# Sliding-window attention, channel mix and gated conv in one launch: seven quarter products for `val`, and the conv's fifth tap by an accumulating DMA

## The chip, the cores and the metric

One core of one Trainium2 chip runs the whole program in one launch. The metric is the device time of the launch in microseconds, the median over several executions. Before the change it is 450.53 us (three executions, 449.9 to 452.18).

## What is computed

Batch 4, 576 tokens a sequence, 8 heads of 64, so rows of 512 numbers. All inputs and outputs are fp32.

```
attn = softmax(q k^T / 8, only the last 64 positions) v          # 4 x 8 x 576 x 64
x    = attn with its heads side by side                          # 4 x 576 x 512
xk   = mu_k * x + (1 - mu_k) * x_prev;  xr likewise with mu_r
h    = relu(xk @ w_k) ** 2                                       # 512 -> 1024
x2   = sigmoid(xr @ w_r) * (h @ w_v)                             # 1024 -> 512
gate = sigmoid(sum over k = 0..4 of conv_w[k] * x2 shifted by 4 - k tokens)
out  = (gate * (x2 @ w_val)) @ w_out                             # both 512 x 512
```

## The kernel before, in words

**Products.** A product of fp32 data is made of three matmuls of fp32r: every operand is split into a high part (a copy in fp32r) and a low part (the operand less its high part), and high x high, low x high and high x low are added up in PSUM. The splits are `split` (high part on ScalarE, L410, or as a cast on VectorE, L411; low part on VectorE, L413) and, for weights, `weight` (L224, L225, L227); a weight comes as 64-bit words that `words` (L198 to L203) turns into fp32 first. All products of 128x512 weights and activations go through `gemm` (L426).

**Stages.** The 2304 tokens of the four sequences stand one behind another and are cut in five blocks (256, then four of 512). Attention works on 20 units (a block and a pair of heads); block by block follow the mix `xm` (L380 to L396), `r_tile` (r, then the sigmoid, L513), `h_pair` (h, relu L472, square L496 and L501, low part L503) and `v_tile`, whose result is multiplied by r (L526) and stored to `x2d` in DRAM (L527). Attention of the next block runs between the products of this one. The last part, called the tail here, takes the sequences one by one: `load` brings x2 of a sequence back as `xb` (L537, issued by SyncE), `prep` splits its two halves of 288 tokens, `gate` makes the conv and its sigmoid, `val_pair` the product with w_val (two banks of 128x288 in a call) and its product with the gate (`gv`, L595), which is split again, `out_pair` the product with w_out, the copy to SBUF (L612) and the store (L613). The four taps k = 1 to 4 are VectorE's (L565), tap 0 is ScalarE's (L563). `xb` and `gate` are double buffered: xb2 takes xb0's place, xb3 that of xb1.

**Order.** Nothing runs in the order in which the code names it. Every step is an entry of `Plan` (L50) with a key, an engine, a cost in ns, a rank and the keys it waits for; `Plan.run` sorts them by rank (the tables RANK and ADJ), picks step after step for the engine that could start first, and so writes one fixed instruction queue for each engine. `any` (L68) lets the planner choose between ScalarE and VectorE. On the chip each queue runs strictly in order. So a change of one cost or one table entry can move instructions anywhere in the program.

Of the kernel before, what the change touches and what calls it, by code (L numbers as in the profile page):

```python
# [19 lines left out]
P = 128  # L20
# [21 lines left out]
ADJ = {('exp', 7): 265, ('mask', 15): -40, ('r', 0, 3): -195, (('w_v', 3), 't'): -390, ('h', 2, 1): 40,  # L42
# [4 lines left out]
       ('eps', 5): 250, ('tp', 4): 100, ('rec', 1): 540, ('mask', 10): -250}  # L47


class Plan:  # L50
# [21 lines left out]
    def run(self):  # L72
# [49 lines left out]
def tile_kernel(ctx, tc, qkh, vh, mu, conv, w_k, w_v, w_r, w_val, w_out, out):  # L122
# [17 lines left out]
    sb = ctx.enter_context(tc.tile_pool(name="sb", bufs=2))  # L140
    sb4 = ctx.enter_context(tc.tile_pool(name="sb4", bufs=4))
# [3 lines left out]
    wr = [w1.tile([P, NF, DM], F32R, name=f"wr{i}") for i in range(2)]  # L145
# [18 lines left out]
    plan = Plan(pg=4, pq=1, pa=2, pb=2, pc=2)  # L164
# [41 lines left out]
    def weight(key, rank, w_dram, dst, nm, bufs, prev=None, sprev=None, after=(), free=(), later=None, used=(), queue="dma"):  # L206
# [11 lines left out]
        else:  # L218
# [7 lines left out]
        op((key, "lo"), "dve", v_ns(n), later, [(key, "hi")],  # L226
           lambda: V.tensor_tensor(out=dst[1], in0=s(), in1=f32(dst[0]), op=ALU.subtract))  # L227
# [9 lines left out]
    def unit(u, r):  # L237
# [14 lines left out]
        def half(tag, shape):  # L252

            if t:
                return tile_(at2, tag, shape)
            if hp % 2 == 0:
                Q["half", tag] = tile_(at2, tag, shape)
            return Q["half", tag][:, hp % 2 * shape[1] // 2:]
# [102 lines left out]
    def wide_x():  # L361
        x = [sbx.tile([P, NF, TB], F32R, tag="x", name=f"x{i}") for i in range(4)]
        for t in range(1, NB):
            X[t] = dict(k=x[:2], r=x[2:])

    def mix(t, g, w, r):
# [8 lines left out]
        def scaled():  # L375

            m = M[k] = sb.tile([P, 2, TB], F32, tag="xm", name=f"xm{t}_{g}{w}") if t else X[0][w][:, 2 * g:2 * g + 2]
# [3 lines left out]
        def scaled_v():  # L381
            m = M[k] = sb.tile([P, 2, TB], F32, tag="xm", name=f"xm{t}_{g}{w}") if t else X[0][w][:, 2 * g:2 * g + 2]
# [23 lines left out]
    def split(key, r, deps, n, src, dst):  # L406
# [5 lines left out]
        op((lo, *key[1:]), "dve", v_ns(n), r + 1, [(hi, *key[1:])],  # L412
           lambda: V.tensor_tensor(out=dst(1), in0=src(), in1=f32(dst(0)), op=ALU.subtract))  # L413
# [44 lines left out]
    def h_pair(t, p, r):  # L458
# [4 lines left out]
        for i in range(2):  # L463
# [3 lines left out]
            def relu(e, i=i):  # L467
                if i == 0:
                    Rk[t, p] = sb.tile([P, 2, TB], F32, tag="rk", name=f"rk{t}_{p}")
# [24 lines left out]
        def hi():  # L494
# [7 lines left out]
        op(("slo", t, p), "dve", v_ns(2 * n), r + 2 * d + 4, [("sq", t, p)],  # L502
           lambda: V.tensor_tensor(out=Ss[t][1][:, f, :n], in0=rk(), in1=f32(Ss[t][0][:, f, :n]), op=ALU.subtract))  # L503

    def r_tile(t, m, r):
# [5 lines left out]
        def sig():  # L511
            Sg[t, m] = sb4.tile([P, TB], F32, tag="sg", name=f"sg{t}_{m}")
# [18 lines left out]
    Xb, Gt, Gv, Vg = {}, {}, {}, {}  # L531

    def load(b, r):
# [5 lines left out]
        last = [("x2lo", b - 2, h) for h in range(2)] + [("tap", b - 2, f, TAPS - 1) for f in range(NF)] if b >= 2 else []  # L539
# [3 lines left out]
    def prep(b, h, r):  # L543

        x = lambda i: X[NB - 1]["kr"[h]][i][:, :, :HS]
        src = lambda: Xb[b][:, :, GAP + h * HS:GAP + (h + 1) * HS]
        last = [("val", b - 1, h, p) for p in range(2)] if b else [("h", NB - 1, m) for m in range(NFF)] if h == 0 \
            else [("r", NB - 1, m) for m in range(NF)]
        split(("x2", b, h), r, [("ldx", b), *last], NF * HS, src, x)

    def gate(b, r):
# [3 lines left out]
        last = [("gv", b - 2, h, p) for h in range(2) for p in range(2)] if b >= 2 else []  # L555
        op(("gbuf", b), "none", 0, r, [("ldx", b), *last], buffer)

        def tap(f, k):
# [5 lines left out]
            else:  # L564
                V.scalar_tensor_tensor(out=g, in0=src, scalar=c, in1=g, op0=ALU.mult, op1=ALU.add)  # L565
        for p in range(2):
            for k in range(TAPS):
                for f in range(2 * p, 2 * p + 2):
                    op(("tap", b, f, k), *(("dve", v_ns(S) + 70) if k else ("act", a_ns(S) + 90)), r + 10 * p,
                       [("gbuf", b), "wc"] + ([("tap", b, f, k - 1)] if k else []), lambda f=f, k=k: tap(f, k))  # L570
            op(("gate", b, p), "act", a_ns(2 * S), r + 10 * p + 5, [("tap", b, f, TAPS - 1) for f in (2 * p, 2 * p + 1)],
               lambda p=p: ACT.activation(out=Gt[b][:, 2 * p:2 * p + 2, :], in_=Gt[b][:, 2 * p:2 * p + 2, :],
                                          func=AF.Sigmoid), table="sig")

    def pair2(key, r, p, m0, x, deps, freed, pool, ring):
# [8 lines left out]
    def val_pair(b, h, p, r):  # L584
        f = slice(2 * p, 2 * p + 2)
        q = 4 * b + 2 * h + p
        name = lambda k, q: (k, q // 4, q // 2 % 2, q % 2)
        pair2(("val", b, h, p), r, p, 0, lambda: [X[NB - 1]["kr"[h]][i][:, :, :HS] for i in range(2)],
              lambda i: [("x2lo", b, h), (("w_val", 2 * p + i), "lo")], ("gv", b, h, p), "pb", "pb")

        def gv():
            if p == 0:
                Gv[b, h] = Q["g", h]
            Vg[b, h, p] = sb.tile([P, 2, HS], F32, tag="xm", name=f"gv{b}_{h}{p}")
            V.tensor_tensor(out=Vg[b, h, p], in0=Ps["val", b, h, p][:, :, :HS],  # L595
                            in1=Gt[b][:, f, h * HS:(h + 1) * HS], op=ALU.mult)
        op(("gv", b, h, p), "dve", v_ns(2 * HS), r + 12,
           [("val", b, h, p), ("gate", b, p), "turn_s", *([name("gv", q - 1)] if q else []),
            *([name("glo", q - 2)] if q >= 2 else [])], gv)
        last = [("out", b - 1, h, q) for q in range(2)] if b else []  # L600
        split(("g", b, h, p), r + 13, [("gv", b, h, p), *last], 2 * HS, lambda: Vg[b, h, p],
              lambda i: Gv[b, h][i][:, f, :])

    def out_pair(b, h, p, r):
        pair2(("out", b, h, p), r, p, NF, lambda: Gv[b, h],
              lambda i: [("glo", b, h, 0), ("glo", b, h, 1), (("w_out", 2 * p + i), "lo")], ("o", b, h, p), "pc", "pc")
        q = 4 * b + 2 * h + p

        def store():
            o = sb.tile([P, 2, HS], F32, tag="rk", name=f"o{b}_{h}{p}")  # L610
# [39 lines left out]
    def staging():  # L650
# [3 lines left out]
        Q["raw"] = [sbx.tile([P, 2048], I32, tag="x", name=f"raw{i}") for i in range(2)] \  # L654
            + [a[:, 1].bitcast(I32) for a in (xr, sr)]
        two = [sbx.tile([P, 2, 1024], F32, tag="x", name=f"s_{i}") for i in range(2)]
        Q["sw"] = [two[i][:, j] for i in range(2) for j in range(2)]
# [17 lines left out]
    def turn():  # L675
# [3 lines left out]
        Q["raw2"] = [own.tile([P, 1024], I32, name=f"rawb{i}") for i in range(2)]  # L679
        Q["s2"] = [own.tile([P, 512], F32, name=f"sb_{i}") for i in range(2)]  # L680
        Q["pb"] = ctx.enter_context(tc.tile_pool(name="pb", bufs=2, space=PSUM, side="right"))

    def turn_s():
# [3 lines left out]
        for i in range(2):  # L687
            Q["g", i] = [own.tile([P, NF, HS], F32R, name=f"g{i}{c}") for c in "hl"]
        Q["pc"] = ctx.enter_context(tc.tile_pool(name="pc", bufs=2, space=PSUM))
# [5 lines left out]
    pieces2 = [(n, p) for n in ("w_val", "w_out") for p in range(4)]  # L695
    for i, (name, p) in enumerate(pieces2):
        w, m = {"w_val": (w_val, 0), "w_out": (w_out, DM)}[name]
        c = P * p
# [74 lines left out]
```

## Time and profile before

| | |
|---|---|
| median of three executions | 450.53 us |
| the profiled execution's own time | 449.83 us |
| its span, first to last instruction | 448.0 us |
| busy: TensorE / VectorE / ScalarE / GpSimd | 430.7 / 304.5 / 241.5 / 17.0 us |
| matmuls of the tail (val, out) | 384 + 384, of 128x288 |
| tail, from the first val matmul to the end | 341.63 to 448.0 us |

The profile is of one execution, which lasted 449.83 us, of which 448.0 us lie between its first and its last instruction. "PE" is TensorE, "DVE" VectorE, "ACT" ScalarE, "POOL" GpSimd, "SP" SyncE. Busy time is a sum over the span; what ends an engine's idle time is named behind an arrow. A row of a timeline merges neighbours of one kind (x84: 84 instructions), and its duration then runs from the first start to the last end. Instructions overlap at their ends, so the step from one start to the next is shorter than the duration of one.

### The profile page before, as it was taken

The page shows a single profiled execution, that of the slowest core. Times are in us where ns is not written, and L with a number is a line of the kernel's source. Part 1 is how long each engine was busy: PE and PEld are TensorE (multiplying, and loading weights), DVE is VectorE, ACT ScalarE, POOL GpSimd, SP SyncE. Part 2 cuts the span into 40 slices and gives each one's busy share as a digit, 9 for nine tenths or more (in the row PEclk, how much of TensorE's full clock was granted, in tenths as well). Part 3 has the DMA queues.
Part 4 walks back from the last instruction along what each step waited for, and adds up shares of the span by engine and source line. Part 5 has one row for each costly group of instructions (what it writes and reads, how often), then busy time and mean ns, then how long its engine had stood idle before and what let it go on. Part 6 is the DMA issues. An engine that isn't in the chain of part 4 may idle for free.

```text
span 448.0 us, 7939 instructions
## 1 busy us (share of the span) xinstructions
PE 430.7 (96%) x3220; PEld 369.5 (82%) x3220; DVE 304.5 (68%) x438; ACT 241.5 (54%) x546; POOL 17.0 (4%) x67
## 2 busy tenths in 40 slices
PE   6889899889999999999999989999999999999996
PEld 4668788668878888888888878888889999999996
DVE  3999899978497149597254266999111999998130
ACT  4799898768555358697239553297100353413121
POOL 2011000001000001001000000000000000000000
PEclk9989999999999999999999999999999999999999
DMA  8996733601131152221120008241133004010122
GB/s 311 407 341 236 283 102 122 214 6 47 48 105 44 72 171 65 89 90 49 47 95 1 0 1 292 96 128 60 22 132 126 28 29 159 26 54 26 48 87 105
DMA packets 16116, 48.90 MB, mean 109 GB/s; under 512 B 1872, under 2 KB 2640, under 8 KB 14800
## 3 DMA queue, kind: packets, MB, share of 16 engines
q1 hardware_dynamic: 15216, 42.10, 27.3%
q10 hardware_dynamic: 864, 6.29, 3.7%
q8 instruction: 25, 0.41, 0.4%
q14 instruction: 11, 0.09, 0.1%
HBM read 38.95 MB, written 9.44 MB: 108 GB/s over the span
## 4 chain that ended last, share of the span: by engine, by line
PE 80%; DVE 12%; DMA 4%; ACT 1%; issue 1%; POOL 0%; ACTq 0%; SPq 0%; POOLq 0%; DVEq 0%
PE h L426 20%; PE v L426 19%; PE out L426 11%; PE val L426 9%; PE r L426 9%; PE qk L277 4%; PE at L343 3%; PE at L330 3%; DMA raw<-w_v 2%; PE r L444 2%; DMA xb<-x2d 1%; DVE s L322 1%; DVE x L413 1%; DVE s L289 1%; DVE s L203 1%
## 5 line engine op out<-in xcount | busy, mean ns | idle before, releaser
L426 PE MATMUL h<-x,wk 128*128 128x512 f32 x384 | 91.0, 393 | 0.0
L426 PEld LDWEIGHTS h<-x,wk 128*128 128x128 f32 x384 | 71.1, 188 | 14.7
L426 PE MATMUL v<-sh,wv 128*128 128x512 f32 x256 | 80.7, 391 | 0.0
L313 ACT ACTIVATE s<-s,m 128x128 f32<-128x128 f32 x144 | 55.7, 388 | 14.6 <-DVE m L307 14.6
L426 PEld LDWEIGHTS v<-sh,wv 128*128 128x128 f32 x256 | 48.1, 188 | 10.2 <-issue 0.2
L426 PE MATMUL val<-x,wk 128*128 128x288 f32 x384 | 53.0, 294 | 0.3 <-DVE gv L595 0.3
L426 PEld LDWEIGHTS val<-x,wk 128*128 128x128 f32 x384 | 51.4, 188 | 0.8 <-DVE gv L595 0.6
L426 PE MATMUL v<-sl,wv 128*128 128x512 f32 x128 | 49.9, 389 | 0.0
L565 DVE SCALAR_TENSOR_TENSOR gate<-xb,wc,gate 128x576 f32<-128x576 f32 x64 | 48.6, 812 | 1.6 <-ACT gate L563 1.6
L426 PE MATMUL r<-x,wr 128*128 128x512 f32 x192 | 47.0, 397 | 0.0
L426 PEld LDWEIGHTS r<-x,wr 128*128 128x128 f32 x192 | 35.2, 188 | 8.1 <-DVE x L413 0.4
L526 DVE TENSOR_TENSOR sg<-v,sg 128x512 f32<-128x512 f32 (+1 forms) x20 | 12.7, 635 | 38.9 <-PE v L426 36.7
L289 DVE SCALAR_TENSOR_TENSOR s<-qk,cap 128x1024 f32<-128x1024 f32 (+1 forms) x24 | 22.5, 952 | 14.7 <-PE qk L277 9.5
L472 ACT ACTIVATE rk<-h 128x512 f32<-128x512 f32 (+1 forms) x36 | 19.9, 556 | 22.4 <-PE h L426 21.9
L503 DVE TENSOR_TENSOR sl<-rk,sh 128x1024 fp32r<-128x1024 f32 x16 | 19.6, 1222 | 15.4 <-ACT rk L501 15.2
L612 ACT ACTIVATE o<-out 128x576 f32<-128x576 f32 (+1 forms) x17 | 10.4, 618 | 36.0 <-PE out L426 26.0
L563 ACT ACTIVATE gate<-xb,wc 128x576 f32<-128x576 f32 x16 | 11.3, 766 | 31.8 <-DMA xb<-x2d 30.7
L426 PEld LDWEIGHTS v<-sl,wv 128*128 128x128 f32 x128 | 24.0, 188 | 4.8
L426 PE MATMUL out<-g0h,wk 128*128 128x288 f32 x128 | 27.4, 295 | 0.0
L330 PE MATMUL at<-ident,s 128*128 128x128 f32 x144 | 22.8, 282 | 4.3 <-DVE s L322 3.2
L313 ACT ACTIVATION_READ_ACCUMULATOR s<-s,m 128x1 f32 x144 | 26.9, 187 | 0.0
L426 PE MATMUL out<-g1h,wk 128*128 128x288 f32 x128 | 26.6, 295 | 0.0
(112 smaller groups left out, 675.2 us busy)
## 6 DMA issues: line engine op xcount, KB each, us to landing
qk<-qk SPq DMA_DIRECT2D x16, 544.0 KB, 4.9
vt<-vh SPq DMA_DIRECT2D x16, 512.0 KB, 4.3
xb<-x2d SPq DMA_DIRECT2D x4, 1152.0 KB, 5.8
out_t<-o SPq DMA_DIRECT2D x15, 288.0 KB, 2.1
x2d<-sg SPq DMA_DIRECT2D x16, 256.0 KB, 2.0
raw<-w_r SPq DMA_DIRECT2D x2, 1024.0 KB, 8.4
raw<-w_k ACTq DMA_DIRECT2D x2, 1024.0 KB, 7.9
raw<-w_v ACTq DMA_DIRECT2D x2, 1024.0 KB, 8.2
```

The lines of the kernel that those rows point to most:

```text
L277: PE.matmul(a["ps"][heads[c % 2], h, c // 2 * P:c // 2 * P + P], lhsT=a["q"][heads[h], c * W:(c + 1) * W], rhs=a["k"][heads[h], c * W:c * ...
L289: V.scalar_tensor_tensor(out=o, in0=ps[:, i:i + j], scalar=D ** -0.5, in1=cap[:, None, :].to_broadcast([P, j, P]), op0=ALU.mult, op1=ALU.min)
L313: ACT.activation(out=s, in_=s, func=AF.Exp, bias=l(0)[:, c:c + 1], accum_out=l(1)[:, c:c + 1])
L330: PE.transpose(a["tp", h][:, c * P:(c + 1) * P], a["s"][:, h * n2 + c, :], ident)
L343: PE.matmul(a["o"][heads[h], c * W:(c + 1) * W], lhsT=a["v"][:, c, heads[h]], rhs=a["pt"][:, h, c * W:(c + 1) * W], start=True, stop=True)
L426: PE.matmul(ps, lhsT=a, rhs=b[:, kt, :], start=(kt == 0 and i == 0), stop=(kt == nk - 1 and i == 2))
L472: ACT.activation(out=o, in_=ps, func=AF.Relu)
L503: lambda: V.tensor_tensor(out=Ss[t][1][:, f, :n], in0=rk(), in1=f32(Ss[t][0][:, f, :n]), op=ALU.subtract))
L526: V.tensor_tensor(out=s, in0=Ps["v", t, m][:, :n], in1=s, op=ALU.mult)
L563: ACT.activation(out=g, in_=src, func=AF.Copy, scale=c)
L565: V.scalar_tensor_tensor(out=g, in0=src, scalar=c, in1=g, op0=ALU.mult, op1=ALU.add)
L612: ACT.activation(out=o[:, i], in_=Ps["out", b, h, p][:, i, :HS], func=AF.Copy)
```

## The change

(a) **val by seven products of quarters.** Per sequence, x2 (its halves of 288 tokens by its two 256-wide halves of features) and w_val are cut in quarters; four sums of x quarters and four differences of weight quarters are formed, and seven quarter products (12 matmuls of 128x288 each) replace the eight of before: 84 matmuls a sequence in place of 96. Two PSUM banks collect them: `u` takes m1, m6, m7 and m4 one on top of the other, `v` takes m2, then m5, then m3. After m1, m6 and m7 the running sum in `u` is copied to SBUF by ScalarE (L684), and VectorE adds it to what `v` holds (`valc`, L713) before the product with the gate (`gv`, L715); the quarter that needs no copy is multiplied straight from PSUM (L718). The splits of a sequence are five in place of two: one 1152 wide, four 576 wide, behind the four sums (L594, high parts L601 on ScalarE or L602 on VectorE, low parts L604). w_val comes in two pieces with four differences of 256 each.

(b) **The fifth tap of sequences 1 to 3** (k = 4): ScalarE scales it into `tt` (L632, two instructions of 576 for each half of the features), and a DMA issued by GpSimd adds the 128x1152 of `tt` (576 KB) to `gate` (L643), six in all. It waits for tap 0 of both features. The taps of VectorE (L626) that follow wait for the DMA. They go from 64 to 52.

(c) w_out goes to the place of w_r instead of beside w_val; the staging tiles are merged. The helper `vg` puts the low parts and sums on VectorE (no step of before's splits changes its engine by it). RANK and ADJ have new numbers, and the planner adds a small bias against VectorE, so the whole order is made anew.

TensorE has 2498 matmuls in place of 2546. The core of the diff (constants, storage and the weight pieces cut):

```diff
+        for p in range(2):
+            fs = (2 * p, 2 * p + 1)
+            for f in fs:
+                op(("tap", b, f, 0), "act", a_ns(S) + 90, r + 10 * p, [("gbuf", b), "wc"], lambda f=f: tap(f, 0))
+            d = [("tap", b, f, 0) for f in fs]
+            for k in by:
+                op(("part", b, p, k), "act", 2 * a_ns(S) + 180, r + 10 * p + 1,
+                   ["turn_s", ("gbuf", b), "wc", *([parts[-2]] if len(parts) > 1 else [])], lambda p=p, k=k: part(p, k))
+                parts.append(("acc", b, p, k))
+                op(parts[-1], "pool", 1000, r + 10 * p + 1, [("part", b, p, k), *d], lambda p=p, k=k: G.dma_start(
+                    out=Gt[b][:, 2 * p:2 * p + 2, :], in_=Z[b, p, k], accum_op=ALU.add), moves=3500)
+                d = [parts[-1]]
...
+        product(0, "m1", A11, B11, "u", True, [], fin(1, 0))
+        copy(0, "m1", 0)
+        product(1, "m2", A12, B21, "v", True, [], fin(0, 0))
+        use(0, 0, r + 7, lambda: Zv("v"), lambda: U[mul, b, 0], [key("m2"), (mul + "u", b, 0)])
+        product(2, "m6", S2, T2, "u", False, [(mul + "u", b, 0), key("m1")])
+        copy(1, "m6", 2)
+        product(3, "m5", S1, T1, "v", True, [], fin(0, 1))
+        product(4, "m7", S3, T3, "u", False, [(mul + "u", b, 1), key("m6")])
+        copy(2, "m7", 4)
+        use(1, 1, r + 25, lambda: Zv("v"), lambda: U[mul, b, 2], [key("m5"), (mul + "u", b, 2)])
+        product(5, "m4", A22, T4, "u", False, [(mul + "u", b, 2)])
+        use(1, 0, r + 31, lambda: Zv("u"), None, [key("m4")])
+        product(6, "m3", S4, B22, "v", False, [fin(1, 1)])
+        use(0, 1, r + 37, lambda: Zv("v"), lambda: U[mul, b, 1], [key("m3"), (mul + "u", b, 1)])
...
+            if u:
+                op(("valc", b, h, p), "dve", v_ns(QN), r, deps,
+                   lambda: V.tensor_tensor(out=u(), in0=ps(), in1=u(), op=ALU.add))
+                vg(("gv", b, h, p), QN, r + 1, [("valc", b, h, p), ("gate", b, p)],
+                   lambda E: E.tensor_tensor(out=g(), in0=u(), in1=g(), op=ALU.mult))
...
-                gemm(Ps[key][:, i, :HS], wk, x(), m0 + 2 * p + i, range(NF), NF)
+                gemm(Ps[key][:, i, :HS], wr, x(), m0 + 2 * p + i, range(NF), NF)
```

Three places of the new order matter for what follows.

ScalarE, where val of the first sequence runs and the second sequence's xb arrives. Before (`gate_3147` is gate1, `xb_3090` xb1):

```order
L513 ACTIVATE sg_3_2963<-r_3_2934 128x512
L563 ACTIVATE gate_3147<-xb_3090,wc 128x576 x3
L410 ACTIVATE g0h<-gv_01_3151 128x576
L563 ACTIVATE gate_3147<-xb_3090,wc 128x576
L410 ACTIVATE g1h<-gv_10_3183 128x576
```

After (`val0m_3006` is bank u of the first sequence, `gate_3097` gate1, `xb_3037` xb1, `xt` the sums):

```order
L601 ACTIVATE x<-xt 128x576 x2
L684 ACTIVATE sgs<-val0m_3006 128x576 x2
L624 ACTIVATE gate_3097<-xb_3037,wc 128x576 x2
L601 ACTIVATE x<-xt 128x576
L684 ACTIVATE sgs<-val0m_3006 128x576
L632 ACTIVATE tt_04_3105<-xb_3037,wc 128x576 x2
L624 ACTIVATE gate_3097<-xb_3037,wc 128x576
```

The copies after m1 and m6 stand ahead of two scalings of xb1 and of a split of a sum of xb1; the copy after m7 stands behind them.

SyncE, at the end of the channel mix. Before, the load of the third sequence (`xb_2966`) stands ahead of the last four stores of x2:

```order
L537 DMA xb_2966<-x2d 128x4x576
L527 DMA x2d<-sg_0_2916 128x512
L527 DMA x2d<-sg_1_2932 128x512
L527 DMA x2d<-sg_2_2947 128x512
L527 DMA x2d<-sg_3_2963 128x512
L537 DMA xb_3090<-x2d 128x4x576
```

After, the same load (`xb_2977`) stands between them, two stores ahead of xb1's (`xb_3037`):

```order
L232 DMA st<-w_out 128x1024 x4
L540 DMA x2d<-sgs 128x512 x2
L569 DMA xb_2977<-x2d 128x4x576
L540 DMA x2d<-sgs 128x512 x2
L569 DMA xb_3037<-x2d 128x4x576
```

It has moved behind two stores, and on VectorE behind the sums of xb0 that it overwrites.

VectorE, where val of the second sequence has begun (after; `gate_2615` is gate0, `val1m` belongs to the second sequence, `xb_2977` is xb2; x2: two of a kind):

```order
L715 TENSOR_TENSOR gate_2615<-sgs,gate_2615 128x2x288
L713 TENSOR_TENSOR sgs<-val1m_3162,sgs 128x576
L604 TENSOR_TENSOR x<-xt,x 128x576
L604 TENSOR_TENSOR x<-xb_2977,x 128x1152
L594 TENSOR_TENSOR xt<-xb_2977 128x576
L426 TENSOR_TENSOR g0l<-gate_2615,g0h 128x576
L594 TENSOR_TENSOR xt<-xt,xb_2977 128x576
L604 TENSOR_TENSOR x<-xt,x 128x576
L713 TENSOR_TENSOR sgs<-val1m_3198,sgs 128x576
L604 TENSOR_TENSOR x<-xt,x 128x576
L426 TENSOR_TENSOR g1l<-gate_2615,g1h 128x576 x2
L626 SCALAR_TENSOR_TENSOR gate_3097<-xb_3037,wc,gate_3097 128x576
```

The last row is the first tap of gate1, of feature block 2, and the first instruction that waits for an accumulating DMA. It stands 26 instructions behind xb1's cast; before, the first two taps of gate1 stood five behind it. The two scalings (L632) that its half of gate1 waits for are ScalarE's eleventh and twelfth instruction behind the copy after m7.

## Rows read from the trace of the kernel before

**Rows 1.** The page, parts 1 and 2: busy times, and TensorE's granted clock by slices.

```profile
PE 430.7 (96%) x3220; PEld 369.5 (82%) x3220; DVE 304.5 (68%) x438; ACT 241.5 (54%) x546; POOL 17.0 (4%) x67
...
PEclk9989999999999999999999999999999999999999
```

**Rows 2.** Stretches: span, busy us (count) of PE, PEld, DVE, ACT, POOL; clock, DMA.

```profile
80.00:100.00 20.00, 16.73 (x170) 13.27 (x164) 17.41 (x25) 15.49 (x45) 1.05 (x7) 1.00 0.38 123
100.00:260.00 160.00, 160.00 (x1194) 130.63 (x1192) 94.77 (x133) 97.34 (x235) 6.27 (x16) 1.00 0.21 65
...
309.00:341.70 32.70, 32.70 (x146) 27.09 (x145) 8.24 (x10) 5.49 (x8) 0.12 (x1) 1.00 0.17 61
341.70:353.20 11.50, 11.16 (x86) 10.93 (x84) 6.85 (x10) 3.39 (x6) 0.11 (x1) 1.00 0.38 127
353.20:444.30 91.10, 91.07 (x684) 90.72 (x684) 65.45 (x91) 27.89 (x37) 0.11 (x1) 1.00 0.16 60
```

**Rows 3.** The chain of work that ended last: start, us, engine and work.

```profile
339.88 1.99 DMA x2d<-sg
342.96 5.93 DMA xb<-x2d
...
421.87 22.41 PE out L426 x168
```

**Rows 4.** TensorE's timeline where the tail begins: start, us, work, idle before.

```profile
341.63 11.22 PE L426 MATMUL val<-x,wk 128*128 128x288 f32 x84
353.19 5.00 PE L426 MATMUL val<-x,wk 128*128 128x288 f32 x36 [0.34 <-DVE gv L595]
```

**Rows 5.** VectorE's timeline, 348.99 to 352.38 and 404.34 us.

```profile
348.99 0.76 DVE L411 CAST x<-xb 128x1152 fp32r<-128x1152 f32 x1 [0.38 <-DMA xb<-x2d]
349.67 0.75 DVE L595 TENSOR_TENSOR gv<-val,gate 128x576 f32<-128x576 f32 x1
350.33 1.35 DVE L413 TENSOR_TENSOR x<-xb,x 128x1152 fp32r<-128x1152 f32 x1
...
404.34 5.91 DVE L565 SCALAR_TENSOR_TENSOR gate<-xb,wc,gate 128x576 f32<-128x576 f32 x8
```

**Rows 6.** ScalarE's timeline, 348.98 to 351.58 us.

```profile
348.98 2.11 ACT L563 ACTIVATE gate<-xb,wc 128x576 f32<-128x576 f32 x3 [28.31 <-DMA xb<-x2d]
351.00 0.67 ACT L410 ACTIVATE g0h<-gv 128x576 fp32r<-128x576 f32 x1
351.58 0.76 ACT L563 ACTIVATE gate<-xb,wc 128x576 f32<-128x576 f32 x1
```

**Rows 7.** SyncE's timeline: issue of loads and stores.

```profile
322.30 0.53 SPq L537 DMA_DIRECT2D xb<-x2d  x1
329.01 13.90 SPq L527 DMA_DIRECT2D x2d<-sg  x4
```

**Rows 8.** VectorE's groups by shape: count, then busy us and mean ns of one.

```profile
L565 DVE SCALAR_TENSOR_TENSOR gate<-xb,wc,gate 128x576 f32<-128x576 f32 x64 | 48.6, 812 | 1.6 <-ACT gate L563 1.6
L413 DVE TENSOR_TENSOR g1l<-gv,g1h 128x576 fp32r<-128x576 f32 x8 | 6.0, 755 | 0.6 <-ACT g1h L410 0.5
L411 DVE CAST g0h<-gv 128x576 fp32r<-128x576 f32 x5 | 2.2, 455 | 9.1 <-PE out L426 9.1
```

**Rows 9.** DMA issues: KB each, median us from issue to landing.

```profile
xb<-x2d SPq DMA_DIRECT2D x4, 1152.0 KB, 5.8
...
raw<-w_r SPq DMA_DIRECT2D x2, 1024.0 KB, 8.4
...
rawb<-w_out SPq DMA_DIRECT2D x4, 512.0 KB, 3.4
```

**Rows 10.** GpSimd's timeline: the same copy of two numbers a partition, twice.

```profile
65.25 0.24 POOL L419 COPY xT<-xT 128x2 f32<-128x2 f32 x1 [6.63 <-DVE xm_0k L396]
...
106.38 1.38 POOL L419 COPY xT<-xT 128x2 f32<-128x2 f32 x1 [6.27 <-DVE xm_0k L396]
```

**Rows 11.** VectorE's timeline at the second of these.

```profile
106.50 1.22 DVE L413 TENSOR_TENSOR x<-xm_0r,x 128x1024 fp32r<-128x1024 f32 x1
```

More of the change, by code (lines that the diff above doesn't have):

```diff
@@ L554, in buffer @@
             Gt[b] = Q["own", b % 2].tile([P, NF, S], F32, tag="gate", name=f"gate{b}")
-        last = [("gv", b - 2, h, p) for h in range(2) for p in range(2)] if b >= 2 else []
+        last = [("glo", b - 2, h, p) for h in range(2) for p in range(2)] if b >= 2 else []
         op(("gbuf", b), "none", 0, r, [("ldx", b), *last], buffer)
@@ L565, in tap, with part @@
                 V.scalar_tensor_tensor(out=g, in0=src, scalar=c, in1=g, op0=ALU.mult, op1=ALU.add)
-        for p in range(2):
[L567 to L571, printed above, removed]
+        def part(p, k):
+            t = Z[b, p, k] = Q["tt"].tile([P, 2, S], F32, tag="tt", name=f"tt{b}_{p}{k}")
+            for i in range(2):
+                c = k * NF + 2 * p + i
+                ACT.activation(out=t[:, i], in_=Xb[b][:, 2 * p + i, k:k + S], func=AF.Copy, scale=wc[:, c:c + 1])
@@ new lines, in gate @@
+        by = BY_DMA if b else ()
+        for p in range(2):
+            fs = (2 * p, 2 * p + 1)
[9 more added lines that the diff above has]
+                d = [parts[-1]]
+            ks = [k for k in range(1, TAPS) if k not in by]
+            for k in ks:
+                for f in fs:
+                    op(("tap", b, f, k), "dve", v_ns(S) + 70, r + 10 * p + 2,
+                       [*d, *([("tap", b, f, k - 1)] if k > 1 else [])], lambda f=f, k=k: tap(f, k))
+            convs[b] = ks[-1]
+            op(("gate", b, p), "act", a_ns(2 * S), r + 10 * p + 5, [("tap", b, f, convs[b]) for f in (2 * p, 2 * p + 1)],
@@ L572, in gate, with seven, product, go @@
                lambda p=p: ACT.activation(out=Gt[b][:, 2 * p:2 * p + 2, :], in_=Gt[b][:, 2 * p:2 * p + 2, :],
                                           func=AF.Sigmoid), table="sig")
+    def seven(mul, b, r, k, a, w, wkeys, turn, use):
+        x = [slots(a, i) for i in range(2)]
+        z = {}
+        key = lambda m: (mul, b, m)
+        has = {A12: A11} if k == "x" else {}
+        def product(i, m, q, t, bank, new, deps, freed=None):
+            def go():
+                if new:
+                    z[bank] = Q[mul].tile([P, 2, TB], F32, tag=bank, name=f"{mul}{b}{m}")
+                for j in range(2):
+                    for kt in range(2):
+                        xs = [v(q)[:, kt * HS:(kt + 1) * HS] for v in x]
+                        ws = [w(c, j)[:, t, kt, :] for c in range(2)]
+                        for e, (lhs, rhs) in enumerate(((ws[0], xs[0]), (ws[0], xs[1]), (ws[1], xs[0]))):
+                            PE.matmul(z[bank][:, j, :HS], lhsT=lhs, rhs=rhs, start=new and kt == 0 and e == 0,
+                                      stop=kt == 1 and e == 2, skip_group_check=not new)
+            op(key(m), "pe", 12 * mm_ns(HS), r + 6 * i, [(k + "lo_", b, has.get(q, q)), *wkeys, turn, *deps], go,
+               ring=(mul + bank, freed) if new else None)
+        def copy(i, m, j):
+            def go(E):
+                o, p = Q[mul + "u"](i), z["u"][:, :, :HS]
+                U[mul, b, i] = o
+                E(o, p)
+            plan.any((mul + "u", b, i), r + 6 * j + 1, [key(m), *used[i]],
+                     ("act", a_ns(QN), lambda: go(lambda o, p: ACT.activation(out=o, in_=p, func=AF.Copy))),
+                     ("dve", v_ns(QN), lambda: go(lambda o, p: V.tensor_copy(o, p))))
+        fin = lambda h, p: (mul + "c", b, h, p)
+        prev = lambda h, p: [({"val": "gv", "out": "outc"}[mul], b - 1, h, p)] if b else []
+        used = [prev(0, 0), prev(0, 1), prev(1, 1)]
+        if mul == "val" and not b:
+            used = [[("x2", NB - 1, m) for m in range(NF)]] * 3
+        Zv = lambda bank: z[bank][:, :, :HS]
+        product(0, "m1", A11, B11, "u", True, [], fin(1, 0))
[12 more added lines that the diff above has]
+        use(0, 1, r + 37, lambda: Zv("v"), lambda: U[mul, b, 1], [key("m3"), (mul + "u", b, 1)])
@@ new lines, in val, with use @@
+    def val(b, r):
+        def use(h, p, r, ps, u, deps):
+            g = lambda: Gt[b][:, 2 * p:2 * p + 2, h * HS:(h + 1) * HS]
+            if u:
[3 more added lines that the diff above has]
+                   lambda E: E.tensor_tensor(out=g(), in0=u(), in1=g(), op=ALU.mult))
+            else:
+                op(("valc", b, h, p), "dve", v_ns(QN), r, [*deps, ("gate", b, p)],
+                   lambda: V.tensor_tensor(out=g(), in0=ps(), in1=g(), op=ALU.mult))
+                op(("gv", b, h, p), "none", 0, r, [("valc", b, h, p)], lambda: None)
+        seven("val", b, r, "x", lambda: Q["xq"], lambda c, j: w2["w_val"](c, j),
+              [(("w_val", j), "lo") for j in range(2)], "turn", use)
@@ L575, in pair2, with gated @@
+    def gated(b, h, p, r):
+        last = [("out", b - 1, h, q) for q in range(2)] if b else []
+        split(("g", b, h, p), r, [("gv", b, h, p), "turn_s", *last], QN,
+              lambda: Gt[b][:, 2 * p:2 * p + 2, h * HS:(h + 1) * HS], lambda i: Q["g", h][i][:, 2 * p:2 * p + 2, :])
     def pair2(key, r, p, m0, x, deps, freed, pool, ring):
@@ L653, in staging @@
         Q["x0"], Q["s0"] = xr[:, 0], sr[:, 0]
[L654 to L657, printed above, removed]
+        w = sbx.tile([P, 4, 2048], F32, tag="x", name="words")
+        Q["raw"] = [a.bitcast(I32) for a in (w[:, 0], w[:, 1], xr[:, 1], sr[:, 1])]
+        Q["sw"] = [w[:, 2 + i, j * 1024:(j + 1) * 1024] for i in range(2) for j in range(2)]
     op("staging", "none", 0, -1100, [], staging)
@@ new lines, in tile_kernel @@
+    for j in range(2):
+        quarter_weights(j, "w_val", j, w_val, ("w_val", 0) if j else None)
+    for i in range(4):
+        prev = ("w_out", i - 2) if i >= 2 else ("w_val", 1)
+        weight(("w_out", i), L + RANK["w2"] + 20 + 10 * i, w_out, [d[:, :, P * i:P * i + P] for d in wr], P,
+               lambda i=i: (Q["raw2"][:, i % 2 * 1024:][:, :1024], Q["s2"][:, i % 2 * 512:][:, :512]), prev, prev, ["turn"],
+               [("r", NB - 1, m) for m in range(NF)])
+    for b in range(B):
+        s = END + 75 * b
+        load(b, L + 10 if b == 0 else s + RANK["ldx"])
+        gate(b, L + 110 if b == 0 else s + RANK["gate"])
+        prep(b, s + RANK["prep"])
+        val(b, s)
@@ L756 @@
         "w_r": piece(inputs["moe_w_r"], 256),
[L757 removed]
+        "w_val": quarters(inputs["moe2_w_val"]), "w_out": piece(inputs["moe2_w_out"], P),
     }
```

200 lines of the change are left out of this document (127 added, 73 removed), and 4 rows, old and new, of the table ADJ.

## The prediction

> **What bounds the kernel now.** I began with the page. TensorE is busy 430.7 of 448.0 us and the other engines are far from it [rows 1]; its granted clock stands at the upper level, 2.4 GHz, in every slice but the first few, so a matmul costs what it costs and the clock is no part of the question. Then the stretches [rows 2]: from 100 to 260 us and from 309 us on TensorE has no idle time to speak of, 0.34 us before 353.2 and 0.03 us after. VectorE in that last stretch works 65.45 of 91.10 us: it has room, but not much. The only other hole that the change could touch is 80 to 100 us, where TensorE works 16.73 of 20. The chain [rows 3] names what comes next if TensorE gets shorter: the last store of x2, the load of xb1 behind it (landing at 342.96 + 5.93 = 348.9), xb1's split, and then val; at the end 22.41 us of out matmuls without a gap. So a matmul taken out of the tail is worth its full step, until VectorE, xb1's arrival or a copy comes later than TensorE does.
>
> **Matmuls removed.** 84 val matmuls run 11.22 us [rows 4], which is 0.133 a step (the records' 294 ns each overlap). 48 fewer: 48 x 0.133 = -6.4 us. TensorE's tail is then 720 steps of 0.133 = 95.8 us; nothing in the other products changes in number.
>
> **New waits of TensorE in the tail.** Before, it waits once for 0.34 us [rows 4]. Now m4 may not start before ScalarE has copied the sum after m7, and that copy stands behind two scalings of xb1 and the high part of xb1's first sum. Step by step: TensorE reaches m4 after 60 matmuls, 341.63 + 60 x 0.133 = 349.6. ScalarE cannot begin the scalings before xb1 is there, 348.98; three take 2.11 [rows 6], so two end at 350.4. VectorE's cast of xb1 takes 0.68 from start to start and the sum then about 0.75 [rows 5], 350.4 as well. High part 0.58, copy 0.67 [rows 6]: 351.7. So TensorE stands 2.1 us, where it had work before. Then val of the second sequence needs bank `v`, which is free when VectorE has reached the last `valc` of the first, behind some eight splits and sums of xb1: I put 0.7 us on it, and 0.4 us on the small hand-overs through two single banks in the other sequences (bounds for both together: 0, and twice the 0.7 with four waits of 0.34 as in [rows 4], 2.8). Together 3.2 us, less the 0.34 of before: +2.9, from +1.8 to +4.6. Every us by which xb1 is later adds one to it.
>
> **VectorE's added work.** Per sequence 4 sums, 3 `valc` and three more splits come in, and 12 taps in all go. The step of a 576-wide instruction of two tensors is 350.33 - 349.67 = 0.67 [rows 5], of a tap 5.91 less the overlap over 8 = 0.727 [rows 5], of a 1152-wide subtraction 1.27 (of the record's 1.35), of a 576-wide cast about 0.37 (0.455 less 0.085). From xb1's cast (349.0) to the first tap of gate1: 23 x 0.67 + 0.68 + 2 x 1.27 = 18.6, so 367.6. From there to the last low part: 36 taps x 0.727 = 26.2, 45 x 0.67 = 30.2, one of 1.27, 6 casts x 0.37 = 2.2, together 59.9: 427.5. Behind the last low part stand 60 out matmuls, 8.0 us, and the last copy and store, 3.7 us (TensorE's last stretch ends at 444.3 of 448.0 [rows 2]): 439.2. TensorE's own sum ends later (below), so VectorE is hidden, with 4 us to spare. That is the cover of all the added work; whole durations in place of steps (0.755, 0.812 [rows 8]) take it away, which is the first rival.
>
> **xb2's load.** It moves on SyncE behind two stores and waits for xb0's sums, from 322.30 [rows 7] to about 335.7: VectorE has some 27 us of work ahead of the last of these sums from 309 on, the splits and sums of xb0 and the last pieces of w_out, by the steps above. The load ends 5.8 us later [rows 9], at 341.5, among the stores (four, issued from 329.01 to 342.9 [rows 7]) and just ahead of xb1's issue at 343.0 [rows 3]: no collision, cost 0. If VectorE is a us or two late in 309 to 341, where it works 8.24 us of 32.7 before [rows 2] and some 28 now, the two loads share the engines and xb1 lands up to 2 us later: upper end +2.
>
> **The accumulating DMA.** Nothing in the trace shows one. Bounds: 3.4 us, a load of 512 KB, and 8.4 us, 1024 KB in the crowded start [rows 9]. I take 5.8, that of xb, whose 1152 KB are what is read here (two times 576). The second one of gate1 is issued when ScalarE has made its `tt`: 12 instructions of 0.58 to 0.70 [rows 6] behind the copy at 351.7, so about 359.5. Its tap comes up at 367.6: 8.1 us are free, and the other five have more. Cost 0; at 12 us it is +3.9, less what VectorE has to spare.
>
> **Before 309 us.** All is replanned. At best the hole of 80 to 100 us closes, -3.3 [rows 2]; at worst the new order opens one, for which I allow +1.5. In the new order three copies and a few mixes leave VectorE ahead of the product that waits there, and six scalings come in, which leaves a small gain; I take -1.
>
> **Sum.** -6.4 + 2.9 - 1 = -4.5. Span 448.0 - 4.5 = 443.5; the profiled execution lasts 449.83, so 445.3. That execution is 0.7 below the median of 450.53; by the median the forecast is **446.0 us**.
>
> **Rivals.**
> 1. *VectorE becomes the bound* (0.17). If it goes by durations rather than steps, the 18.6 become 20.8 and the 59.9 become 67.2: last low part 437.0, end 437.0 + 8.0 + 3.7 = 448.7 against 448.0, so 451.2: no change. For it: it works 78 to 80 of some 95 us now. Against it: neighbours in the timeline do overlap by 0.085 [rows 5].
> 2. *Descriptor writing on GpSimd is held up by VectorE, and the DMA comes late* (0.12): slower. In this trace a copy of two numbers on GpSimd takes 0.24 us, but 1.38 when it starts beside a subtraction of 1.22 on VectorE [rows 10, 11], and ends with it: 106.38 + 1.38 = 107.76 against 106.50 + 1.22 = 107.72. From 349.0 to 367.6 VectorE now runs such instructions without a gap. If a DMA's writing is held for as long, it is done only when VectorE itself stands and waits at the tap: 5.8 us for each of three sequences, 17.4; 427.5 + 17.4 + 8.0 + 3.7 = 456.6 span, 459.1 by the median. It decides from 9 us of such waits on (427.5 + 9 + 11.7 = 448.2). Against it: the small copy was held by one instruction and no longer. The Trainium skill, SBUF — State Buffer, "SBUF: two separate sides", has the same trap: GpSimd cannot write descriptors while VectorE runs an instruction in a two-port mode, an fp32 copy above all, and a DMA of 620 ns took about 3100 so. Its section "Who interferes with whom" lets instructions with two inputs block only GpSimd's reads, and infers that descriptor writing is untouched; [rows 10, 11] agree on the reads. By it only casts would count here, and the few between scaling and tap last 0.455 each [rows 8]: nothing to see. No row of before shows which holds.
> 3. *The replanned first part gains more* (0.11): the hole of 80 to 100 us closes and no copy is late: about 443.
>
> **Chances.** A measurement of this kernel tells about 0.5% from no change, so 448.3 and 452.8 are the borders. Forecast 0.60, rivals 0.17, 0.12, 0.11. Faster: 0.60 + 0.11 = 0.71; same: 0.17; slower: 0.12. The range goes from the third rival, less a little, to the near end of the first and second: 442.5 to 450.5; outside lie the second and half of the first, 0.2.
>
> **What would show it.** Right: val matmuls 336, one wait of TensorE of about 2 us near 350 before m4, put down to ScalarE's copy (L684); VectorE near 80 us busy behind 353 with its last low part 8 to 10 us before TensorE's end; taps (L626) of gate1 without a wait for a DMA; xb1 landing at 349. Wrong: VectorE idle before L626 and a DMA named (rival 2), TensorE waiting for VectorE's low parts (L426, L604) again and again (rival 1), xb1 landing after 350 (the price of xb2's move), or a difference before 309 us of over 2 us either way.

## The result and the profile after

The changed kernel takes 446.2 us by the median (six executions, 444.8 to 448.11) against 450.85 for the kernel before beside it: a ratio of 0.989, 95% interval 0.987 to 0.992. The forecast was 446.0. Two more sets of six on the same kernel, beside experiments, gave 446.16 and 445.71, with ratios of 0.991 and 0.988. The profiled execution lasted 444.80 us, its span is 443.0.

The page, parts 1 and 2, of the changed kernel:

```profile
PE 424.6 (96%) x3172; PEld 362.1 (82%) x3172; DVE 326.6 (74%) x474; ACT 266.2 (60%) x584; POOL 22.4 (5%) x69
...
PEclk9999999999999999999999999999999999999999
```

Against [rows 1], TensorE has 48 instructions and 6.1 us less, VectorE 22.1 us more, ScalarE 24.7 more. Then TensorE's timeline: the first val matmuls, and all of its waits from there on (start, us, work, idle before).

```profile
338.51 8.15 PE L672 MATMUL val0m<-x,wk 128*128 128x288 f32 x60
348.67 3.46 PE L672 MATMUL val0m<-x,wk 128*128 128x288 f32 x24 [2.00 <-ACT sgs L684]
354.10 6.79 PE L672 MATMUL val1m<-x,wk 128*128 128x288 f32 x48 [0.38 <-DVE sgs L713]
...
387.60 1.87 PE L672 MATMUL val2m<-x,wk 128*128 128x288 f32 x12 [1.06 <-ACT sgs L684]
```

The wait of 2.0 us stands at m4 of the first sequence, where [rows 4] show work without a break. ScalarE's timeline there:

```profile
345.91 1.44 ACT L624 ACTIVATE gate<-xb,wc 128x576 f32<-128x576 f32 x2 [1.76 <-DMA xb<-x2d]
347.39 0.68 ACT L601 ACTIVATE x<-xt 128x576 fp32r<-128x576 f32 x1
347.98 0.63 ACT L684 ACTIVATE sgs<-val0m 128x576 f32<-128x576 f32 x1
```

It is the forecast chain: xb1 lands, two scalings, a high part, and only then the copy that m4 waits for. The third wait is the same thing once more: the copy after m7 of the third sequence stands behind the high part of xb3, which lands late. SyncE's timeline, then ScalarE's:

```profile
339.79 0.53 SPq L569 DMA_DIRECT2D xb<-x2d  x1
...
378.83 0.53 SPq L569 DMA_DIRECT2D xb<-x2d  x1
```

```profile
385.85 1.17 ACT L601 ACTIVATE x<-xb 128x1152 fp32r<-128x1152 f32 x1 [2.36 <-DMA xb<-x2d]
386.92 0.63 ACT L684 ACTIVATE sgs<-val2m 128x576 f32<-128x576 f32 x1
```

xb1 is issued at 339.79 and xb3 only at 378.83 (371.97 before, when the tail began 3 us later), since VectorE's taps of gate1 have to be done first. The accumulating DMAs, on the page and on GpSimd's timeline, and VectorE's first tap behind one:

```profile
gate<-tt POOLq DMA_DIRECT2D x6, 576.0 KB, 4.8
```

```profile
350.26 1.02 POOL L643 DMA_DIRECT2D gate<-tt  x1 [11.42 <-ACT tt L632]
356.39 0.85 POOL L643 DMA_DIRECT2D gate<-tt  x1 [5.11 <-ACT tt L632]
```

```profile
363.25 1.42 DVE L426 TENSOR_TENSOR g1l<-gate,g1h 128x576 fp32r<-128x576 f32 x2
364.59 0.81 DVE L626 SCALAR_TENSOR_TENSOR gate<-xb,wc,gate 128x576 f32<-128x576 f32 x1
```

The median is 4.8 us from issue to landing, within the bounds of 3.4 and 8.4, and no tap waits: from the second DMA's issue to its tap VectorE gives it 364.59 - 356.39 = 8.2 us (8.1 forecast), of which 3.4 are left over.

Where the time came from, by stretches of the two profiles: the first val matmul starts at 338.51 instead of 341.63 (-3.12), and from there to the end it is 443.0 - 338.51 = 104.49 instead of 448.0 - 341.63 = 106.37 (-1.88). The first of these is not all the change's. These rows are the stretch from 20 to 40 us, of the kernel before and then of the changed one (columns as in [rows 2], the clock third from the end):

```profile
20.00:40.00 20.00, 17.57 (x158) 14.40 (x157) 19.88 (x30) 17.51 (x41) 3.25 (x7) 0.91 0.90 342
```

```profile
20.00:40.00 20.00, 17.02 (x179) 13.58 (x175) 19.88 (x30) 18.52 (x42) 2.52 (x7) 1.00 0.94 350
```

The granted clock averages 0.91 in the one: 20 x 0.09 / 0.5 = 3.6 us at the lower of its two levels (1.2 GHz), none in the other. Both kernels have executions of either kind. In nine later profiles of the changed kernel, or of one whose order is equal to it up to the tail, val begins at 339.71 to 340.55 where that fall is there (seven) and at 338.90 and 338.98 where it is not. So with the fall in both kernels the first part gave 1.1 to 1.9 us. Without it there is the profile of experiment 2, whose TensorE has the order of before up to the tail and begins val at 340.83: 1.9 to 2.3 us. The rest of the 3.12, 1 to 2 us, goes with the clock of one execution.

What the first part gave is in the hole of [rows 2], whichever clock an execution had. TensorE works 18.44 of the 20 us from 80 to 100 us where it worked 16.73, so 1.7 us of idle time are gone (16.68 in experiment 2, 18.45 in experiment 6). The changed kernel:

```profile
80.00:100.00 20.00, 18.44 (x165) 14.45 (x164) 18.95 (x31) 15.49 (x46) 1.63 (x7) 1.00 0.36 117
```

### The profile page after: what moved, and what is told of

Same layout as the page of the kernel before. It is cut to its first block, busy times and chain, and to the rows that moved or that the text cites. A ratio compares the mean times of both kernels' runs of the same rounds, so it can differ in the third digit from the quotient of the medians.

```text
span 443.0 us, 7915 instructions
## 1 busy us (share of the span) xinstructions
PE 424.6 (96%) x3172; PEld 362.1 (82%) x3172; DVE 326.6 (74%) x474; ACT 266.2 (60%) x584; POOL 22.4 (5%) x69
## 4 chain that ended last, share of the span: by engine, by line
PE 71%; DVE 20%; issue 3%; DMA 3%; ACT 2%; POOL 1%; ACTq 0%; POOLq 0%
PE h L439 20%; PE v L439 20%; PE r L439 9%; PE out L439 8%; PE qk L289 3%; PE at L355 3%; DMA xb<-x2d 3%; PE at L342 3%; PE val3m L672 3%; DVE x L604 2%; DVE m L319 2%; DVE words L215 2%; DVE s L301 2%; DVE s L334 1%; DVE xt L594 1%
## 5 line engine op out<-in xcount | busy, mean ns | idle before, releaser
L626 DVE SCALAR_TENSOR_TENSOR gate<-xb,wc,gate 128x576 f32<-128x576 f32 x52 | 39.5, 810 | 0.0
L539 DVE TENSOR_TENSOR sgs<-v,sgs 128x512 f32<-128x512 f32 (+1 forms) x20 | 12.7, 635 | 25.7 <-PE v L439 25.7
L439 PE MATMUL out<-g0h,wr 128*128 128x288 f32 x128 | 27.4, 295 | 0.0
L439 PE MATMUL out<-g1h,wr 128*128 128x288 f32 x128 | 27.2, 295 | 0.0
L355 PEld LDWEIGHTS at<-pt,vt 128*64 128x64 f32 x576 | 19.9, 137 | 8.6 <-issue 3.8
L355 PE MATMUL at<-pt,vt 128*64 128x64 f32 x576 | 23.6, 226 | 2.3 <-ACT pt L348 1.9
L409 DVE SCALAR_TENSOR_TENSOR xm<-xT,omu,xm 128x320 f32<-128x320 f32 (+6 forms) x56 | 25.4, 516 | 0.0
L319 DVE TENSOR_REDUCE m<-s 128x8 f32<-128x1024 f32 (+1 forms) x20 | 22.1, 1106 | 2.0 <-POOL s L311 1.9
```

What stands on the lines that cost most here:

```text
L319: V.tensor_reduce(out=l(0), in_=a["s"], axis=AX.X, op=ALU.max, negate=True)
L355: PE.matmul(a["o"][heads[h], c * W:(c + 1) * W], lhsT=a["v"][:, c, heads[h]], rhs=a["pt"][:, h, c * W:(c + 1) * W], start=True, stop=True)
L409: V.scalar_tensor_tensor(out=m, in0=xT[:, f, lo:hi], scalar=omu[:, c:c + 1], in1=m, op0=ALU.mult, op1=ALU.add)
L439: PE.matmul(ps, lhsT=a, rhs=b[:, kt, :], start=(kt == 0 and i == 0), stop=(kt == nk - 1 and i == 2))
```

## The experiments

**1 and 7: the seven products without the DMA tap.** First with the order planned anew, then with every queue in the changed kernel's order.

```diff
-BY_DMA = (4,)
+BY_DMA = ()
```

> The changed kernel with all taps back on VectorE (no scaling into tt, no accumulating DMA); the planner orders it anew with the same tables. Theory (the seven products leave VectorE only 3 to 4 us to spare in the tail, so they need the tap taken off it): 12 taps x 0.727 = 8.7 us more on VectorE, 4 to 5 of them come out at the end: 449 to 451 us, with TensorE waiting for low parts (L426, L604) in the tail. Rival (TensorE's matmuls alone set the end, the DMA's tap only buys room that nothing needs): 446 us, within 0.7 of the changed kernel.

457.38 us, against 449.37 for the kernel before: ratio 1.017 (1.013 to 1.020). Slower than either theory. Is it the order? In the seventh, tap 4 is an instruction of VectorE ahead of tap 1, the scalings and DMAs are empty steps:

```diff
-                       [*d, *([("tap", b, f, k - 1)] if k > 1 else [])], lambda f=f, k=k: tap(f, k))
+                       [*d, *([("tap", b, f, k - 1)] if k > 1 else [])],
+                       lambda f=f, ks=(*by, k) if k == 1 else (k,): [tap(f, k) for k in ks])
```

> The changed kernel, every queue in the changed kernel's order, but the fifth taps are twelve instructions of VectorE that stand beside the tap k = 1 of the same feature; ScalarE's twelve scalings and the six DMAs are left out. Theory (VectorE has 3 to 4 us to spare, and xb3's load waits for gate1's taps): 8.7 us of taps less the spare, 4 to 6 us slower than the change: 450 to 452. If the order was the reason for the 457 us of the first experiment (planned anew by tables made for the other kernel), this stays under 452; if VectorE's load was, it is at 455 or more.

456.08 us beside 446.16 for the change: 9.9 us for twelve taps that take 8.7, and over my 450 to 452. So it is VectorE's load, not the order. TensorE's timeline at its longest wait, and three stretches around it:

```profile
381.77 3.25 PE L672 MATMUL val2m<-x,wk 128*128 128x288 f32 x12 [3.22 <-DVE gate L718]
```

```profile
378.00:382.00 4.00, 0.78 (x6) 0.54 (x5) 3.96 (x7) 1.70 (x2) 0.00 (x0) 0.82 0.19 74
382.00:386.00 4.00, 4.00 (x17) 4.00 (x18) 2.77 (x5) 1.64 (x3) 0.11 (x1) 0.50 0.17 24
386.00:390.00 4.00, 4.00 (x27) 4.00 (x27) 3.96 (x7) 2.99 (x5) 0.00 (x0) 0.83 0.90 341
```

TensorE's waits in the tail add up to 9.2 us in this profile, 3.5 in the change's profile beside it: +5.7, which puts VectorE's spare at 8.7 - 5.7 = 3.0, near my 3 to 4. What my theory left out is the clock. It falls to its lower level in the wait and is there for 4 x 0.18 / 0.5 + 4 + 4 x 0.17 / 0.5 = 6.8 us; a matmul of 128x288 then comes every 0.24 us (17 in the 4 us of the middle row) instead of every 0.133, and 12 val matmuls take 3.25 us, 1.87 in the change. That is 6.8 x (1 - 0.133 / 0.24) = 3.0 us at most, less what of it lies in the wait itself. About a microsecond of the 9.9 is in neither.

**2: the DMA tap alone, in the kernel before** (the diff of `gate` put into it, `val_pair` unchanged).

> The kernel before with only the fifth tap of sequences 1 to 3 by ScalarE and the accumulating DMA; val by eight products as before. Theory (TensorE bounds the tail of before, VectorE is hidden): no change, 450 to 451.5 us; VectorE's busy time falls by 12 x 0.81 = 9.7 us, its idle time grows by as much. Rival 1 (relief of VectorE is where the change's gain is from): 447 to 449 us. Rival 2 (the DMA's writing is held up by VectorE): over 453 us, with VectorE idle before a tap.

449.30 us against 449.37, ratio 1.000 (0.998 to 1.002): no change. The page's busy line shows VectorE at 296.5 us, 8.0 less than in [rows 1] (9.7 expected):

```profile
PE 429.3 (96%) x3220; PEld 368.4 (82%) x3220; DVE 296.5 (66%) x425; ACT 248.8 (56%) x559; POOL 22.2 (5%) x73
```

In the tail each part alone gives nothing or costs time; only the two together gain. The tap is the room that the seven products need.

**8: the DMAs made late.** GpSimd reads two numbers of `tt` and clears a scratch tile twelve times before each.

```diff
+        def late(p, k):
+            w = Q["tt"].tile([P, S], F32, tag="w", name=f"w{b}_{p}")
+            G.tensor_copy(w[:, 0:2], Z[b, p, k][:, 1, S - 2:S])
+            for _ in range(12):
+                G.memset(w, 0.0)
+            G.dma_start(out=Gt[b][:, 2 * p:2 * p + 2, :], in_=Z[b, p, k], accum_op=ALU.add)
```

> The changed kernel with a wait put ahead of each accumulating DMA: GpSimd reads two numbers of the scaled tile and then clears a scratch tile of 576 twelve times (some 6 to 8 us), so that each DMA starts that much later. Theory (the first DMA lands 3.4 us before VectorE comes to its tap, the others earlier still): 3 to 5 us of delay show at the first tap, VectorE's spare takes most of it, 446.5 to 450 us. Rival (the DMAs have 8 us and more to spare, as forecast): no change, 446. Rival 2 (every DMA's landing sets VectorE's pace): 455 or more.

457.8 us (453.32 to 460.08), 11.6 above the change. GpSimd's timeline, then VectorE's:

```profile
360.09 1.02 POOL L638 DMA_DIRECT2D gate<-tt  x1
360.79 4.44 POOL L635 COPY w<-tt 128x2 f32<-128x2 f32 x1
365.29 7.59 POOL L637 MEMSET w<- 128x576 f32 x12
372.83 0.85 POOL L638 DMA_DIRECT2D gate<-tt  x1
```

```profile
364.44 0.75 DVE L604 TENSOR_TENSOR x<-xt,x 128x576 fp32r<-128x576 f32 x1
365.11 0.75 DVE L718 TENSOR_TENSOR sgs<-val1m,sgs 128x576 f32<-128x576 f32 x1
...
377.64 0.82 DVE L626 SCALAR_TENSOR_TENSOR gate<-xb,wc,gate 128x576 f32<-128x576 f32 x1 [9.78 <-DMA gate<-tt]
```

Counted from the first val matmul (340.55 here), the second DMA came (372.83 - 340.55) - (356.39 - 338.51) = 14.4 us later than in the change, since the delays of two DMAs queue up on GpSimd, and VectorE stood 9.78 us at the first tap. My theory was wrong because I counted one delay and not two behind each other. The time is in the range of this experiment's rival 2, but its mechanism held for one DMA only: no other tap waits. A late DMA does become VectorE's wait, TensorE then waits 8.42 us behind it, and the clock is down again (0.61 between 380.5 and 386 us). What does *not* happen is that VectorE holds up the writing of descriptors: in the change the issue of the second DMA takes 0.85 us on GpSimd, and its data is there before VectorE, busy from end to end, comes to the tap. Here the same issue takes 0.85 us with VectorE standing still. In both profiles a DMA lands 4.8 us behind its issue by the median. The copy of two numbers, which reads SBUF, took 4.44 us. It ends at 365.23, when VectorE has come to its first instruction since 360.79 that takes one of its inputs from PSUM (L718, at 365.11); all between take both from SBUF. The Trainium skill, SBUF — State Buffer, "Who interferes with whom", separates the two in just this way, and these rows agree.

**3: the first part's order alone**, the changed kernel's ranks and adjustments for everything ahead of the tail in the kernel before.

> The kernel before with the changed kernel's ranks, adjustments and bias for everything ahead of the tail; the tail's work and ranks as before. Theory (the new order of the first part is worth more than the 1 us that was forecast): 447.5 to 449 us, the first full-width r matmul near 83.5 us in place of 86.2. Rival (the 3 us that the profiles differ by before 309 us are the granted clock of one execution, 0.91 between 20 and 40 us in the one and 1.00 in the other): 450 to 451 us by the median.

447.91 against 449.37, ratio 0.996 (0.994 to 0.998): 1.5 us less by the medians, 1.7 by the ratio. In its profile val begins at 339.67, 2.0 us ahead of before, with the same fall of the clock in both. The theory, at a little over half of the 3.1 us.

**4, 5 and 10: the waits taken away.** In the fourth, ScalarE's copies after m7 (first and third sequence) stand ahead of what they waited behind; in the fifth, two sums of VectorE as well. Each is a list of emitted steps that are put behind another, together with what depends on them; nothing else moves. The list of the fifth, whose first two entries are the fourth's (the code that moves the steps is left out):

```diff
+MOVED = [(("valu", 0, 2), [("tap", 1, 0, 0), ("tap", 1, 1, 0), ("xhi_", 1, 3)]),
+         (("valu", 2, 2), [("xhi_", 3, 0)]),
+         (("valc", 0, 1, 1), [("xlo_", 1, 3)]),
+         (("valc", 0, 0, 1), [("xlo_", 1, 2), ("xsum", 1, 5), ("gv", 0, 1, 1)])]
```

> The changed kernel with two edits of ScalarE's order and no other: the copy after m7 of the first sequence ahead of the two scalings of xb1 and the high part of xb1's first sum, the copy after m7 of the third sequence ahead of the split of xb3. Theory (these copies are what TensorE waits for): its waits of 2.0 us at 348.7 and 1.06 at 387.6 go, and 2 to 3 us come out at the end: 443.3 to 444.5 us. Rival (the split of xb1 that now comes 0.6 us later, or VectorE, holds TensorE a few us later instead): 445.5 to 446.5 us, with a new wait for VectorE's low parts in val of the second sequence.

446.02 us (0.991 of before, 0.988 to 0.995; no run of the change stood beside it): the rival, with VectorE's sums in place of its low parts. TensorE's timeline:

```profile
349.18 1.86 PE L694 MATMUL val0m<-x,wk 128*128 128x288 f32 x12 [0.74 <-ACT sgs L706]
352.54 1.86 PE L694 MATMUL val0m<-x,wk 128*128 128x288 f32 x12 [1.51 <-DVE sgs L735]
...
356.55 6.80 PE L694 MATMUL val1m<-x,wk 128*128 128x288 f32 x48 [0.55 <-DVE sgs L735]
```

2.0 became 0.74, which the copy itself takes with its hand-overs, and the next wait, for VectorE's sum of m5, took over.

> The fourth experiment's kernel with two edits of VectorE's order: the sum of m5 (valc) of the first sequence ahead of the low part of xb1's first sum, and the sum of m3 ahead of xb1's next split and sum. Theory (in the fourth experiment TensorE's wait only moved from ScalarE's copy to these two sums, 1.51 and 0.55 us): both go, the wait of 0.74 before m4 stays, and 1.5 to 2 us come out against the fourth experiment and against the change: about 444 where the change is at 446. Rival (VectorE then has its work for the second sequence late by as much, and a low part of xb1 or a tap holds TensorE): within 0.7 us of the change.

444.99 us where the change gave 446.16 beside it. In its profile five waits are left, 0.74, 0.35, 0.54, 0.41 and 0.31, together 2.35 us for 3.5, and the tail is 444.7 - 340.51 = 104.2 us for 104.6. Three of the five (0.35, 0.41 and 0.31) are for VectorE's sums and products. The next set was to settle the 1.2 us:

> The fifth experiment's kernel once more, beside the change, to settle whether it is the faster one. Theory (a wait of 0.74 us in place of 2.0, with no execution in which the clock falls behind it): 444.5 to 445.5, 1 to 1.5 us below the change, and no execution above 447. Rival: level with the change.

445.54 beside 445.71 for the change: ratios to the kernel before 0.987 (0.983 to 0.990) and 0.988 (0.984 to 0.991). The two are level within what this measures, and so are their tails (443.1 - 338.98 = 104.1 us here, 104.2 in experiment 11). A better version is not shown.

**6 and 11: the change again**, beside experiments 4 to 10.

> The changed kernel itself, unedited, beside the others of this set: 445.5 to 446.5 us if the kernel before is at 450, its tail (from the first val matmul to the end) 104.3 us whatever the first part took.

446.16 us. Tail in its profile 444.3 - 339.71 = 104.6.

> The changed kernel unedited beside the two others: 446 us, with some executions at 448 whose granted clock is about 0.992.

445.71 us (445.41 to 446.68), without an execution at 448. Tail in its profile 444.7 - 340.47 = 104.2.

**9: the wait before m4 lengthened** by two idle ScalarE instructions on a tile that GpSimd clears, to see whether it is behind the change's executions of 448 us, whose mean clock is 0.992.

```diff
+                if (b, i) == (0, 2):
+                    w = Q["tt"].tile([P, S], F32, tag="w", name="w")
+                    G.memset(w, 0.0)
+                    for _ in range(2):
+                        ACT.activation(out=w, in_=w, func=AF.Copy)
```

> The changed kernel with two idle copies of a scratch tile (576 wide) on ScalarE ahead of the copy after m7 of the first sequence, so that TensorE's wait there grows from 2.0 to some 3.2 us. Theory (a wait of this length brings TensorE's clock to its lower level for 3.4 us, at 2 us it does so in some executions only, and these are the change's 448 us ones): the granted clock falls behind this wait in nearly every execution, 1.2 us of wait and 1.7 us of clock: 448.5 to 450 us, and the spread gets smaller. Rival (the falls of the clock have nothing to do with the wait): 447 to 447.8 us, clock by execution as in the change.

447.62 us (446.99 to 447.99) beside 445.71: 1.9 more, as the rival had it, and clocks of 0.994 to 0.996. The wait grew to 3.05 us and the clock behind it stayed at its upper level:

```profile
350.99 3.46 PE L672 MATMUL val0m<-x,wk 128*128 128x288 f32 x24 [3.05 <-ACT sgs L689]
```

My theory fell. In the profiles of experiments 1 and 8 the clock did fall behind waits of 1.87 and 1.86 us at the same place, and the same 24 matmuls took 4.98 us. The first of them:

```profile
348.92 4.98 PE L672 MATMUL val0m<-x,wk 128*128 128x288 f32 x24 [1.87 <-ACT sgs L684]
```

So the length of this one wait does not decide it. What does was not found, nor where the clock falls in the change's executions of 448 us, of which there is no profile.

## Why the prediction was right, step by step

- **Matmuls removed, -6.4.** Right in kind and size: 336 val matmuls at the same step.
- **New waits in the tail, +2.9.** The main one was right in place, cause and size: m4, ScalarE's copy behind xb1's scalings, 2.00 us for 2.1. The v bank cost 0.38 for 0.7. The mis-sized term is "0.4 us on the small hand-overs": the same copy in the third sequence stood behind xb3's high part, 1.06 us. I had looked at xb1's arrival and not at xb3's, which waits for gate1's taps on the fuller VectorE. In steps of TensorE, the tail is 338.51 to 439.06 = 100.55 us for 720 matmuls, 100.55 - 720 x 0.133 = 4.8 above them, 0.5 before (102.63 - 768 x 0.133): +4.3 where I had +2.9, near the upper bound of 4.6. Idle rows add up to 3.44 of it; a restart behind a wait costs some more than its row says. The wait before m4 is not worth its 2.0 us by itself: with it at 0.74 (experiments 4, 5 and 10) the tail takes 104.1 to 104.2 us, where the change takes 104.2 to 104.6, because VectorE's sums hold TensorE next.
- **The tail's sum, -3.5.** -6.4 + 4.3, and 0.2 for an end of 3.9 in place of 3.7: -1.9, as the two profiles have it.
- **VectorE hidden with 4 us to spare.** It is hidden. The last low part is done at 429.7 (427.5 forecast), but xb1's cast came 3.1 us earlier than there, so by the prediction's own count this is 5.3 us late. Some 4 us of that are waits of VectorE, 2.62 + 0.34 us of them for TensorE shortly before the end; its work itself was right to about 1 us. Experiment 7 puts the spare at 3.0. First rival wrong by little: twelve taps more and it is the bound.
- **xb2's load, 0.** Issued at 331.47, 4 us earlier than forecast; xb1 landed as reckoned, 7.3 us behind the first val matmul (345.85 - 338.51; 348.98 - 341.63 before).
- **Accumulating DMA, 0.** Right. It takes 4.8 us for 5.8; the second one was issued 10.5 us behind xb1's cast as reckoned, the tap came 18.7 behind it (18.6). Rival 2 did not come about.
- **Before 309, -1.** Right in kind, the hole of 80 to 100 us, and too small: 1.7 us of idle time are gone there, and experiment 3 measures 1.5 to 1.7. The 3.1 us of the two profiles would have misled: the clock of one execution is in them. That "the clock is no part of the question" was wrong to this extent.

Two terms were mis-sized on opposite sides: the waits by 1.4 us, the first part by some 0.7. The stretches, like against like, make -1.9 and about -1.7, so -3.6, where I had -4.5. That the median came out 0.2 us from the forecast is therefore partly luck: about a microsecond that I did not reckon with made up for what my sum had too much. The medians of the three sets are 4.65, 4.35 and 5.54 below the kernel before beside them. The profiled execution of before, 449.83 us, is itself 1.0 below its median of 450.85, so that microsecond probably lies in executions of before that have no profile. How often the clock falls does not explain it: executions of the same mean clock, 0.996, differ by 4.3 us beside experiment 6 (medians of 450.37 and 446.05) and by 5.1 beside experiment 11 (451.25 and 446.19). Where it goes stays open.

## What to carry to other kernels

A cut of matmuls on a saturated TensorE is worth its full step only as long as nobody else is made to work for it: here the cut without the relief of VectorE made the kernel 1.7% slower, and the relief without the cut gave nothing. Look for the one instruction of another engine that the new product waits for, then for what stands ahead of it in its queue; this one wait was read off the order and three rows to 0.1 us, and its twin two sequences on was missed. Taking the longest wait away need not help: the next one in line took its place. Before two profiles are split into stretches, compare their granted clock stretch by stretch.

## What was not expected of the hardware

- A wait costs more than itself when the clock falls with it: TensorE stood 3.22 us in experiment 7 and 6.8 us at 1.2 GHz came with it; yet it stood 3.05 us in experiment 9 and the clock stayed up.
- A GpSimd instruction that reads SBUF can be held for many VectorE instructions (six in experiment 8), not for one: 4.44 us for a copy of two numbers a partition, where [rows 10] had 1.38. Issuing an accumulating DMA is not held: 0.84 to 1.02 us in all twelve issues of the change's profile and experiment 8's.
